# A three-stage decode kernel on one Trainium2 core: decode operations spread over three engines, a new tabulated order, and places for the attention steps of later blocks

## The chip, the cores and the metric

The kernel runs on one core of a Trainium2 chip. The engines are TensorE (PE, matmuls; PEld is its weight load), VectorE (DVE), ScalarE (ACT), GpSimd (POOL) and SyncE (SP, which issues all DMA transfers here). The metric is device time in microseconds, from runs of the whole program: a median of 605.21 us in three runs before the change (604.71 to 607.05).

## The reference

A chunked, decaying linear attention gives x of 3072 tokens by 256, and two feed-forward nets follow:

```
for c in chunks:                       # per batch (4) and head (8), 768 positions
    cum = cumsum(log(a));  M = (C @ B^T) * exp(cum_i - cum_j) * causal
    y   = M @ x + (C @ state) * exp(cum)
    state = exp(sum(log a)) * state + B^T (x * exp(cum_last - cum))
x = x.reshape(3072, 256)
x = ((x @ w1) * (x @ w2)) @ w3 @ w_out      # 256 -> 1024 -> 1024 -> 256
x = max(x @ w_in, 0)                        # 256 -> 2048
out = (x * x) @ w_out2                      # 2048 -> 256
```

The weights are float64 in memory; the rest is float32.

## The kernel before

**Tiles and stages.** The 3072 tokens are 8 blocks f of 384 positions. Attention works on 16 units u of four heads and 384 positions (four chunks of 96); block f needs units 2f (even) and 2f+1 (odd). Of a unit the kernel makes: decay (four scans on DVE, one a head, L297), lw (the last decays, L309), bd (POOL, two kinds of instruction, L315 and L322: B times decays, and the decays of the state), cb and gain (PE, L373 and L331: scores C B^T and the gain of the state), m 0 to 3 (DVE, L384: scores times decays, one a head), state (DVE, L344), carry (ACT, L355: copies the state beside x), y (PE, L391), x and xl (ACT L411, DVE L418: the result split into a high and a low part, xth and xtl). The scores of heads 0 and 1 lie in two PSUM tiles cb, those of head 2 in cbw, a buffer of the ring w that feed-forward products (pw) use too and that has three buffers, and those of head 3 in yu, of which there is one. Products of float32 are made as three matmuls (L150) from high and low parts.

**A block** has an up phase ph_a of 8 steps m and a phase ph_h of 16. In a step of ph_a stand two ab products (x w1 and x w2, 6 matmuls each), copy (ACT), mul (DVE, pr), the high part (ACT, s3h), the low part (DVE, s3l), and x2 products of three steps before. wc is the product of w3 and w_out, made once on PE (L554, 16 steps of four matmuls); x2 is pr times wc. In a step of ph_h stand the h products (x2 w_in, 6 matmuls), relu and the high part of the square (ACT), sq (the square, POOL but ACT in block 0), the low part qlo (DVE, tile s3l), and the o products of three steps before.

**Decode.** The weights come as 44 pieces of 512 KB (load, SP, L233): wo1 0 to 3 (w_out), w3 0 to 15, w1 and w2 0 to 3, wi 0 to 7 (w_in), wo 0 to 7 (w_out2). Pieces 0 and 2 of w1 and w2 are their first half of columns, 1 and 3 the second. Each piece passes high (ACT, L245), low (POOL, L249) and join (DVE, L260), which make float32 of the two words; pieces of w1, w2, wi and wo then pass hi (ACT, L267) and lo (POOL, L271), which split them. Loads wait for one of nine raw buffers, which a join frees.

**Order.** For blocks 0 and 1, units 0 to 5 and all decoding, each operation is entered in a plan with its engine and its dependencies, and the table ORDER, written out by hand in the file, sets the order in which all are issued (Plan.run). For blocks 2 to 7 the order is that of the loops: a counter of slots goes up by one in each step m of both phases (24 slots a block), and run_fill issues, in the step's middle, whatever was put at this slot. Units 6 to 15 are put there: an even unit from slot 0 of the block before the one that needs it, an odd one from slot 8, both with the same steps at 0 to 14 slots behind:

```
    for u in range(EARLY, NU):
        for i, f in unit_steps(u):
            fill.setdefault(BEGIN[u] + i, []).append(f)
```

Of the kernel before, what the change touches and what calls it, by code (L numbers as in the profile page):

```python
# [5 lines left out]
F32 = mybir.dt.float32  # L6
# [40 lines left out]
BEGIN = {u: (u // 2 - 1) * (M1 + M2) + 8 * (u % 2) for u in range(EARLY, NU)}  # L47

ORDER = [
# [30 lines left out]
class Plan:  # L80
# [9 lines left out]
    def run(self, order):  # L90
        names, done = list(self.ops), set()
        assert sorted(order) == list(range(len(names)))
        for n in order:
            _, after, fn, _, _ = self.ops[names[n]]
            assert all(d in done for d in after), (names[n], [d for d in after if d not in done])
            fn()
            done.add(names[n])
# [3 lines left out]
def mixer_kernel(ctx, tc, a, bct, xb, cst, *rest):  # L101
# [42 lines left out]
    def f32(t):  # L144
        return t.bitcast(F32)
# [678 lines left out]
```

## Time and profile before

| | |
|---|---|
| median of three runs | 605.21 us (604.71 to 607.05) |
| the profiled execution | 609.12 us |
| its span, first to last instruction | 607.0 us |
| busy PE, DVE, ACT, POOL | 566.3, 317.4, 279.5, 206.5 us |
| PE's granted clock, mean over the span | 0.974 |

Durations and waits below are of the profiled execution. A busy share is a mean over stages: the first hundred microseconds, with loads and decoding, and the blocks behind them have different limits. PE's durations overlap, since matmuls are pipelined; what one costs is the distance between two starts. An idle time is shown in brackets with what ended it. A granted clock of 1.00 is 2.4 GHz and one of 0.50 is 1.2 GHz.

### The profile page before, as it was taken

Reading aid. Unit: us, or ns where it says so; the run is one execution under the profiler, and the core shown is the slowest. Engines: PE = TensorE matmul, PEld = TensorE weight load, DVE = VectorE, ACT = ScalarE, POOL = GpSimd, SP = SyncE. Lnnn points to the kernel's source line nnn. Section 1 sums busy time; section 2 is a strip of 40 time slices with the busy share of each in tenths; the row PEclk is TensorE's granted clock in tenths of the full one; section 3 lists DMA queues with packets and bytes.
Section 4 is the critical chain, followed back from the end, with each engine's and each line's share of the span. In section 5 each row is a group of like instructions: output and inputs, shape, how many; then the busy total and the mean of one; then the engine's idle time right before and its main releaser. Section 6 shows DMA issues by size and latency. Waiting matters only on the chain. (4 is left out here: it accounts for less than half of the span.)

```text
span 607.0 us, 11321 instructions
## 1 busy us (share of the span) xinstructions
PE 566.3 (93%) x4376; PEld 536.6 (88%) x4376; DVE 317.4 (52%) x564; ACT 279.5 (46%) x586; POOL 206.5 (34%) x279
## 2 busy tenths in 40 slices
PE   3589999899999998999989998999989998999997
PEld 1477788899999998999889998999879998999997
DVE  4798898453433446635373446535383446523331
ACT  2456654794344434453255424443255424443443
POOL 3778968440034112531063113421053113420242
PEclk7589999899999999999999999999999999999999
DMA  7998865201120000220022100220021200000000
GB/s 204 326 329 283 264 198 166 85 2 44 62 66 1 26 2 4 77 80 27 1 80 64 42 1 23 58 79 26 2 79 50 57 1 2 1 1 27 0 2 26
DMA packets 21020, 43.51 MB, mean 72 GB/s; under 512 B 7608, under 2 KB 10920, under 8 KB 20968
## 3 DMA queue, kind: packets, MB, share of 16 engines
q1 hardware_dynamic: 20968, 42.81, 22.4%
q8 instruction: 34, 0.56, 0.4%
q14 instruction: 18, 0.15, 0.1%
HBM read 39.55 MB, written 3.25 MB: 71 GB/s over the span
## 5 line engine op out<-in xcount | busy, mean ns | idle before, releaser
L509 POOL TENSOR_TENSOR q<-r 128x384 f32<-128x384 f32 x112 | 100.3, 900 | 274.9 <-ACT r L501 256.6
L516 DVE TENSOR_TENSOR s3l<-q,s3h 128x384 fp32r<-128x384 f32 x128 | 80.2, 633 | 139.4 <-POOL q L509 106.2
L150 PE MATMUL acc<-s3h,wo 128*128 128x384 f32 x512 | 133.4, 342 | 0.0
L501 ACT ACTIVATE r<-pw 128x384 f32<-128x384 f32 x128 | 62.1, 487 | 113.3 <-PE pw L150 112.6
L150 PEld LDWEIGHTS acc<-s3h,wo 128*128 128x128 f32 x512 | 92.8, 189 | 1.7
L150 PE MATMUL pw<-x2h,wih 128*128 128x384 f32 x256 | 87.5, 342 | 6.9 <-DVE la L384 4.6
L150 PE MATMUL acc<-s3l,wo 128*128 128x384 f32 x256 | 86.8, 339 | 0.6 <-DVE s3l L516 0.6
L150 PE MATMUL pw<-x2h,wil 128*128 128x384 f32 x256 | 86.7, 339 | 0.0
L150 PE MATMUL pw<-x2l,wih 128*128 128x384 f32 x256 | 85.2, 340 | 0.0
L467 DVE TENSOR_TENSOR pr<-pw,asb 128x384 f32<-128x384 f32 x64 | 35.6, 556 | 75.0 <-PE pw L150 73.8
L513 ACT ACTIVATE s3h<-r 128x384 fp32r<-128x384 f32 x128 | 67.1, 525 | 9.2 <-PE acc L150 4.6
L473 ACT CAST s3h<-pr 128x384 fp32r<-128x384 f32 x64 | 32.8, 513 | 71.2 <-DVE pr L467 68.0
L150 PEld LDWEIGHTS pw<-x2h,wih 128*128 128x128 f32 x256 | 48.2, 188 | 9.1 <-DVE la L384 6.2
L463 ACT COPY asb<-pw 128x384 f32<-128x384 f32 x64 | 30.7, 479 | 49.4 <-PE pw L150 49.3
L297 DVE TENSOR_TENSOR_SCAN la<-la,cs 112x384 f32<-112x384 f32 x48 | 50.3, 1054 | 0.3 <-DMA la<-az 0.3
L150 PEld LDWEIGHTS acc<-s3l,wo 128*128 128x128 f32 x256 | 48.3, 189 | 1.3 <-DVE s3l L516 1.0
L150 PEld LDWEIGHTS pw<-x2h,wil 128*128 128x128 f32 x256 | 48.4, 189 | 0.0
L150 PEld LDWEIGHTS pw<-x2l,wih 128*128 128x128 f32 x256 | 48.2, 189 | 0.0
L476 DVE TENSOR_TENSOR s3l<-pr,s3h 128x384 fp32r<-128x384 f32 x64 | 36.7, 574 | 20.1 <-ACT s3h L473 20.0
L150 PE MATMUL acc<-s3l,wch 128*128 128x384 f32 x128 | 43.4, 339 | 1.4 <-DVE s3l L476 1.4
L150 PE MATMUL pw<-xth,w2h 128*128 128x384 f32 x128 | 44.0, 344 | 0.2
L150 PE MATMUL acc<-s3h,wch 128*128 128x384 f32 x128 | 43.9, 343 | 0.0
(85 smaller groups left out, 1031.4 us busy)
## 6 DMA issues: line engine op xcount, KB each, us to landing
la<-az SPq DMA_DIRECT2D x12, 679.0 KB, 4.7
rawl<-in_wo SPq DMA_DIRECT2D x10, 512.0 KB, 5.0
rawe<-in_w3t SPq DMA_DIRECT2D x9, 512.0 KB, 6.5
xa<-in_xb SPq DMA_DIRECT2D x16, 288.0 KB, 5.3
rawl<-in_w3t SPq DMA_DIRECT2D x7, 512.0 KB, 5.9
out_t<-o SPq DMA_DIRECT2D x16, 192.0 KB, 1.9
rawl<-in_w_in SPq DMA_DIRECT2D x5, 512.0 KB, 5.5
rawl<-in_w SPq DMA_DIRECT2D x5, 512.0 KB, 7.3
```

The source lines that it names most:

```text
L150: nc.tensor.matmul(ps, lhsT=w[i == 1], rhs=x[i == 2], start=first and i == 0, stop=last and i == 2)
L297: nc.vector.tensor_tensor_scan(la[:, 0:TB], src[:, 0:TB], cs, 0.0, ALU.mult, ALU.add)
L463: nc.scalar.copy(ab[m], ab.pop((m, 0)))
L467: nc.vector.tensor_tensor(pr, ab.pop((m, 1)), ab[m], op=ALU.mult)
L473: nc.scalar.copy(pt[f, m][0], ab[m])
L476: nc.vector.tensor_tensor(pt[f, m][1], ab.pop(m), f32(pt[f, m][0]), op=ALU.subtract)
L501: nc.scalar.activation(hr[m], hp.pop(m), AF.Relu)
L509: nc.gpsimd.tensor_tensor(q, hr[m], hr[m], op=ALU.mult)
L513: nc.scalar.activation(qt[f, m][0], hr[m], AF.Square)
L516: nc.vector.tensor_tensor(qt[f, m][1], hr.pop((m, 0)), f32(qt[f, m][0]), op=ALU.subtract)
```

## The change

Three things change together. A table MOVED names, for operations of the plan that have more than one possible engine, which it is: low may be on POOL, ACT or DVE, hi on ACT or DVE, lo on POOL or DVE, carry on ACT or POOL, sq on POOL or ACT. By it low goes to ACT 21 times and to DVE 10 times, lo 13 times and hi 4 times to DVE, carry 3 times to POOL; of block 0's squares 4 go to POOL, of block 1's 11 to ACT. ORDER is another table of the same 803 operations. And the steps of units 6 to 15 are seventeen single ones, with a table AT for even and one for odd units that gives each its slot, counted from the start of the same block.

The diff; of the tables a line stands:

```diff
@@ -44,36 +44,59 @@
 PLANNED = 2
-BEGIN = {u: (u // 2 - 1) * (M1 + M2) + 8 * (u % 2) for u in range(EARLY, NU)}
 ORDER = [
-    7, 95, 19, 258, 0, 255, 107, 287, 8, 9, 251, 260, 288, 261, 264, 253, 282, 96, 97, 265, 263, 279, 20, 21, 10, 259, 11, 98, 256, 108, 109, 292, 254,
...
+]
+
+
+MOVED = {
+    5: 1, 17: 2, 21: 2, 33: 1, 41: 1, 45: 1, 57: 1, 61: 1, 65: 1, 77: 2, 81: 1, 85: 1, 91: 1, 97: 1, 99: 1, 100:
...
+}
+
+
+AT = [
+    [0, 1, 3, 5, 5, 6, 7, 7, 7, 8, 9, 9, 11, 13, 14, 14, 14],
+    [6, 6, 13, 13, 14, 16, 18, 18, 19, 19, 19, 20, 20, 22, 22, 22, 23],
 ]
@@ -91,9 +114,12 @@
         for n in order:
-            _, after, fn, _, _ = self.ops[names[n]]
+            eng, after, fn, _, _ = self.ops[names[n]]
             assert all(d in done for d in after), (names[n], [d for d in after if d not in done])
-            fn()
+            if isinstance(eng, tuple):
+                fn(eng[MOVED.get(n, 0)])
+            else:
+                fn()
             done.add(names[n])
@@ -244,9 +272,12 @@
         nc.scalar.activation(z, z, AF.Prelu, scale=2.0 ** -112, alpha=2.0 ** 32)
-    def dec_low(key):
-        t = words[key]
-        nc.gpsimd.tensor_scalar(t[:, :, 0], t[:, :, 0], 0.876 * 2.0 ** -29, 0.49, ALU.mult, ALU.add)
+    def dec_low(key, eng):
+        t = words[key][:, :, 0]
+        if eng == "ACT":
+            nc.scalar.activation(t, t, AF.Copy, scale=0.876 * 2.0 ** -29, bias=0.49)
+        else:
+            on[eng].tensor_scalar(t, t, 0.876 * 2.0 ** -29, 0.49, ALU.mult, ALU.add)
     def dec_join(key):
@@ -261,14 +292,17 @@
         spare.append(slot.pop(key))
-    def dec_hi(key):
+    def dec_hi(key, eng):
         if key in (("wo", 0), ("wo", 4)):
             to_wo(key[1] // 4)
-        nc.scalar.copy(split_to(key)[0], stage[key].bitcast(F32))
-
-    def dec_lo(key):
+        if eng == "ACT":
+            nc.scalar.copy(split_to(key)[0], stage[key].bitcast(F32))
+        else:
+            on[eng].tensor_copy(split_to(key)[0], stage[key].bitcast(F32))
+
+    def dec_lo(key, eng):
         hi, lo = split_to(key)
-        nc.gpsimd.tensor_tensor(lo, stage.pop(key).bitcast(F32), f32(hi), op=ALU.subtract)
+        on[eng].tensor_tensor(lo, stage.pop(key).bitcast(F32), f32(hi), op=ALU.subtract)
     un = {}
@@ -426,20 +461,22 @@
     def unit_steps(u):
-
-
         return [
-            *((h, lambda h=h: u_decay(u, h)) for h in range(HG)),
-            (4, lambda: (u_lw(u), u_bd(u))),
-            (7, lambda: (u_cb(u), u_gain(u))),
-            (8, lambda: (u_m(u, 2), u_m(u, 3))),
-            (9, lambda: (u_state(u), u_m(u, 0))),
-            (10, lambda: (u_m(u, 1), u_carry(u))),
-            (12, lambda: u_y(u)),
-            (13, lambda: (u_loads(u + 2), u_x(u))),
-            (14, lambda: u_xl(u)),
+            *(lambda h=h: u_decay(u, h) for h in range(HG)),
+            lambda: u_lw(u),
+            lambda: u_bd(u),
+            lambda: (u_cb(u), u_gain(u)),
+            lambda: u_m(u, 2),
+            lambda: u_m(u, 3),
+            lambda: u_state(u),
+            lambda: u_m(u, 0),
+            lambda: u_m(u, 1),
+            lambda: u_carry(u),
+            lambda: u_y(u),
+            lambda: u_loads(u + 2),
+            lambda: u_x(u),
+            lambda: u_xl(u),
         ]
-
     pt = {}
@@ -500,10 +537,10 @@
         nc.scalar.activation(hr[m], hp.pop(m), AF.Relu)
-    def h_sq(f, m):
+    def h_sq(f, m, eng="POOL"):
         q = hr[m, 0] = sb.tile([128, FB], F32, tag="s2", name="q")[:, 0:FBS[f]]
-        if f == 0:
+        if eng == "ACT":
             nc.scalar.activation(q, hr[m], AF.Square)
@@ -603,7 +640,7 @@
         op(("high", key), "ACT", [("load", key)], lambda key=key: dec_high(key))
-        op(("low", key), "POOL", [("load", key)], lambda key=key: dec_low(key))
+        op(("low", key), ("POOL", "ACT", "DVE"), [("load", key)], lambda e, key=key: dec_low(key, e))
         ends = [("join", k) for k in pieces if k not in LAST] if key in LAST and key[0] == "wo" else []
@@ -613,8 +650,8 @@
                     after += [("hi", ("wo", key[1] // 4 * 4))]
-            op(("hi", key), "ACT", after, lambda key=key: dec_hi(key))
-            op(("lo", key), "POOL", [("hi", key)], lambda key=key: dec_lo(key), frees=[("v", ("join", key))])
+            op(("hi", key), ("ACT", "DVE"), after, lambda e, key=key: dec_hi(key, e))
+            op(("lo", key), ("POOL", "DVE"), [("hi", key)], lambda e, key=key: dec_lo(key, e), frees=[("v", ("join", key))])
     for f in range(2):
@@ -646,7 +683,7 @@
         op(("state", u), "DVE", [("cb", u)] + prev("carry") + prev("state"), lambda: u_state(u))
-        op(("carry", u), "ACT", [("state", u)], lambda: u_carry(u))
+        op(("carry", u), ("ACT", "POOL"), [("state", u)], lambda e: u_carry(u, e))
         op(("y", u), "PE", [("carry", u)] + [("m", u, h) for h in range(HG)], lambda: u_y(u),
@@ -674,7 +711,7 @@
             op(("relu", f, m), "ACT", [("h", f, m, 1)], lambda m=m: h_relu(f, m), ["s1"], [("w", ("h", f, m, 0))])
-            op(("sq", f, m), "POOL" if f else "ACT", [("relu", f, m)], lambda m=m: h_sq(f, m), ["s2"], [("s1", ("relu", f, m))])
+            op(("sq", f, m), ("POOL", "ACT")[::1 if f else -1], [("relu", f, m)], lambda e, m=m: h_sq(f, m, e), ["s2"], [("s1", ("relu", f, m))])
             op(("qhi", f, m), "ACT", [("relu", f, m)], lambda m=m: h_hi(f, m), ["s3"], [("s1", ("relu", f, m))])
@@ -705,8 +742,8 @@
     for u in range(EARLY, NU):
-        for i, f in unit_steps(u):
-            fill.setdefault(BEGIN[u] + i, []).append(f)
+        for i, f in zip(AT[u % 2], unit_steps(u)):
+            fill.setdefault((u // 2 - 1) * (M1 + M2) + i, []).append(f)
     def ph_a(f, tail):
```

**PE at the start**, from the first scan's inputs on (rows: the decays spread over the partitions; wo1v and ve: wc's inputs; bd_97 and la: of unit 0). Before:

```order
L284 MATMUL rows<-al,sel 112x388 x8
L554 MATMUL acc<-wo1v,ve 128x256 x4
L373 MATMUL cb<-ct,bt_103 112x96 x2
L373 MATMUL cbw<-ct,bt_103 112x96
L373 MATMUL yu<-ct,bt_103 112x96
...
L331 MATMUL yu<-xa,bd_97 32x32 x16
L554 MATMUL acc<-wo1v,ve 128x256 x4
L391 MATMUL yu<-la,xa 32x96 x16
L284 MATMUL rows<-al,sel 112x388 x3
```

The same place after the change:

```order
L318 MATMUL rows<-al,sel 112x388 x8
L408 MATMUL cb<-ct,bt_103 112x96 x2
L408 MATMUL cbw<-ct,bt_103 112x96
L408 MATMUL yu<-ct,bt_103 112x96
...
L365 MATMUL yu<-xa,bd_97 32x32 x16
L426 MATMUL yu<-la,xa 32x96 x16
L318 MATMUL rows<-al,sel 112x388 x3
L591 MATMUL acc<-wo1v,ve 128x256 x8
```

The whole of unit 0's cb, gain and y moved ahead of the first wc step, where one step stood before and one between.

**POOL in the first 30 us** (bd and w2s: of units 0 and 1; rawl and rawe: low; w2l: lo). Before:

```order
L271 TENSOR_TENSOR w2l<-v,w2h 128x512
L315 TENSOR_TENSOR bd_97<-xa,la 96x256
L322 COPY w2s_99<-la 16x4 x4
L249 TENSOR_SCALAR rawl<-rawl 128x512 x5
L315 TENSOR_TENSOR bd_98<-xa,la 96x256
L322 COPY w2s_100<-la 16x4 x4
L249 TENSOR_SCALAR rawe<-rawe 128x512 x3
```

After:

```order
L349 TENSOR_TENSOR bd_97<-xa,la 96x256
L356 COPY w2s_99<-la 16x4 x4
L349 TENSOR_TENSOR bd_98<-xa,la 96x256
L356 COPY w2s_100<-la 16x4 x4
L280 TENSOR_SCALAR rawe<-rawe 128x512
L280 TENSOR_SCALAR rawl<-rawl 128x512
L390 COPY xa<-st_101 16x128 x4
L280 TENSOR_SCALAR rawl<-rawl 128x512 x3
```

Both units' bd moved to the front, low words between them to other engines, and the carry of unit 0 came in.

**DVE around the end of block 2's up phase** (pr and the s3l made from it: the last steps of that phase; x2l: its result; la<-cbw, la<-yu, la<-cb: m 2, 3 and 0 or 1 of the even unit; la<-la,cs: scans of the odd one; st: state; s3l<-q: qlo). Before:

```order
L467 TENSOR_TENSOR pr<-pw,asb 128x384
L476 TENSOR_TENSOR s3l<-pr,s3h 128x384
L489 TENSOR_TENSOR x2l<-acc,x2h 128x384 x2
L384 TENSOR_TENSOR la<-cbw,la 112x384
L384 TENSOR_TENSOR la<-yu,la 112x384
L297 SCALAR_TENSOR_TENSOR la<-la,cs 112x384
L516 TENSOR_TENSOR s3l<-q,s3h 128x384
L344 SCALAR_TENSOR_TENSOR st_101<-st_101,w2s_99,yu 128x32 x4
L384 TENSOR_TENSOR la<-cb,la 112x384
L297 SCALAR_TENSOR_TENSOR la<-la,cs 112x384
L516 TENSOR_TENSOR s3l<-q,s3h 128x384
L384 TENSOR_TENSOR la<-cb,la 112x384
```

After:

```order
L331 SCALAR_TENSOR_TENSOR la<-la,cs 112x384 x2
L513 TENSOR_TENSOR s3l<-pr,s3h 128x384
L504 TENSOR_TENSOR pr<-pw,asb 128x384
L419 TENSOR_TENSOR la<-cbw,la 112x384
L419 TENSOR_TENSOR la<-yu,la 112x384
L513 TENSOR_TENSOR s3l<-pr,s3h 128x384
L526 TENSOR_TENSOR x2l<-acc,x2h 128x384 x2
L378 SCALAR_TENSOR_TENSOR st_101<-st_101,w2s_99,yu 128x32 x4
L553 TENSOR_TENSOR s3l<-q,s3h 128x384
L419 TENSOR_TENSOR la<-cb,la 112x384 x2
L553 TENSOR_TENSOR s3l<-q,s3h 128x384 x4
L331 SCALAR_TENSOR_TENSOR la<-la,cs 112x384 x2
```

The reads of cbw and yu moved ahead of x2l, and the scans moved out from between the even unit's steps, two ahead of the last steps of the up phase and two behind four qlo.

## Rows read from the trace of the kernel before

**Rows 1.** The page: the span and the number of instructions.

```profile
span 607.0 us, 11321 instructions
```

**Rows 2.** Windows: length, busy us (instructions) of each engine, granted clock, DMA.

```profile
0.00:15.00 15.00, 5.86 (x14) 2.15 (x14) 6.24 (x16) 4.12 (x6) 5.19 (x23) 0.78 0.73 203
15.00:30.00 15.00, 8.51 (x77) 6.13 (x78) 10.83 (x21) 6.68 (x11) 11.11 (x20) 0.50 0.95 326
30.00:60.00 30.00, 27.76 (x233) 22.62 (x232) 26.28 (x50) 18.35 (x36) 23.53 (x28) 0.90 0.91 305
60.00:90.00 30.00, 27.26 (x298) 23.32 (x297) 27.77 (x43) 17.91 (x36) 23.98 (x21) 1.00 0.72 231
90.00:104.42 14.42, 12.99 (x128) 11.97 (x126) 12.28 (x18) 7.11 (x14) 12.05 (x15) 1.00 0.52 161
104.42:603.60 499.18, 483.88 (x3642) 470.38 (x3632) 233.99 (x420) 224.86 (x484) 130.62 (x175) 1.00 0.11 34
```

The order of its columns is length; PE, PEld, DVE, ACT, POOL; PE's clock, the DMA engines' share, GB/s.

**Rows 3.** Waits of PE from 120 to 600 us: total, times, longest.

```profile
PE yu L391 <- DVE la L384: 5.2, 5, 1.0
PE pw L150 <- DVE la L384: 4.6, 5, 0.9
PE yu L373 <- issue: 2.5, 5, 0.5
```

**Rows 4.** Timeline of PE in block 2: start, length, instruction, [idle before it].

```profile
233.54 0.44 PE L150 MATMUL pw<-x2h,wih 128*128 128x384 f32 x1 [0.92 <-DVE la L384]
...
240.75 0.86 PE L391 MATMUL yu<-la,xa 112*32 112x96 f32 x30 [1.04 <-DVE la L384]
```

**Rows 5.** Timeline of DVE in block 2.

```profile
232.94 0.55 DVE L384 TENSOR_TENSOR la<-cbw,la 112x384 f32<-112x384 f32 x1
...
240.06 0.55 DVE L384 TENSOR_TENSOR la<-cb,la 112x384 f32<-112x384 f32 x1
...
248.40 0.54 DVE L418 TENSOR_TENSOR xtl<-yu,xth 128x384 fp32r<-128x384 f32 x1
```

**Rows 6.** Timeline of PE at the first h products of block 0.

```profile
103.06 0.34 PE L373 MATMUL cb<-ct,bt 16*112 16x96 f32 x2
...
104.42 0.45 PE L150 MATMUL pw<-x2h,wih 128*128 128x384 f32 x1
...
109.64 0.45 PE L150 MATMUL pw<-x2h,wih 128*128 128x384 f32 x1 [2.30 <-ACT r L501]
109.92 0.34 PE L150 MATMUL pw<-x2h,wil 128*128 128x384 f32 x1
110.10 0.34 PE L150 MATMUL pw<-x2l,wih 128*128 128x384 f32 x1
```

**Rows 7.** Groups by line and form: busy us, mean ns; idle time before, releasers.

```profile
L297 DVE TENSOR_TENSOR_SCAN la<-la,cs 112x384 f32<-112x384 f32 x48 | 50.3, 1054 | 0.3 <-DMA la<-az 0.3
L249 POOL TENSOR_SCALAR rawl<-rawl 128x512 uint32<-128x512 uint32 x27 | 25.6, 949 | 9.5 <-DMA rawl<-in_w3t 3.3 <-DMA rawl<-in_wo 2.0 <-DMA rawl<-in_w 1.4
L245 ACT ACTIVATE rawl<-rawl 128x512 f32<-128x512 f32 x27 | 18.2, 679 | 21.9 <-DMA rawl<-in_wo 8.1 <-DMA rawl<-in_w 5.5 <-DMA rawl<-in_w3t 4.8
L260 DVE SCALAR_TENSOR_TENSOR v<-rawl 128x512 uint32<-128x512 uint32 x17 | 15.7, 921 | 5.7 <-POOL rawl L249 2.9 <-POOL wo L271 2.5 <-POOL w1l L271 0.3
L271 POOL TENSOR_TENSOR wo<-v,wo 128x512 fp32r<-128x512 f32 x8 | 11.3, 1418 | 13.5 <-ACT wo L267 7.2 <-DVE s3l L516 6.3
L572 DVE TENSOR_TENSOR wcl<-acc,wch 128x512 fp32r<-128x512 f32 x4 | 2.6, 677 | 0.0
```

**Rows 8.** Timelines of DVE and POOL at 87 us.

```profile
87.95 1.46 DVE L260 SCALAR_TENSOR_TENSOR v<-rawl 128x512 uint32<-128x512 uint32 x1
...
87.56 1.30 POOL L271 TENSOR_TENSOR wil<-v,wih 128x512 fp32r<-128x512 f32 x1 [1.57 <-ACT wih L267]
```

**Rows 9.** DMA issues on the page: count, KB of one, us to landing.

```profile
rawl<-in_w SPq DMA_DIRECT2D x5, 512.0 KB, 7.3
```

More of the change, by code (lines that the diff above doesn't have):

```diff
@@ L142, in mixer_kernel @@
     bt = [const.tile([128, NCH, TA], F32, name=f"bt{i}") for i in range(2)]
+    on = {"POOL": nc.gpsimd, "DVE": nc.vector}
     def f32(t):
@@ L347, in u_state, with u_carry @@
             )
-    def u_carry(u):
+    def u_carry(u, eng="ACT"):
         d = un[u]
@@ L353, in u_carry @@
         c0 = NCH * ((u // 2) % 2)
+        copy = nc.scalar.copy if eng == "ACT" else on[eng].tensor_copy
         for h in range(HG):
-            nc.scalar.copy(
+            copy(
                 d["xa"][T:TA, h * NCH * D:(h + 1) * NCH * D].rearrange("p (c d) -> p c d", d=D),
```

66 rows, old and new, of tables (MOVED, ORDER) are left out of this document.

## The prediction

> **What bounds the kernel now.** Read first the windows by stage [rows 2]. From 104.42 us, where TensorE (PE) starts the first product of block 0's second feed-forward (the h products), to its last matmul it is busy 483.9 of 499.2 us at full clock: in that stretch only PE's own work and its 15.3 us of idle time count, and VectorE (DVE), ScalarE (ACT) and GpSimd (POOL) are at 47, 45 and 26%. Before 104.42 it is another kernel: PE idles 15.6 of the first 30 us, runs at a granted clock of 0.50 from 15 to 30 us, and later has short holes, while DVE is busy 26.3, 27.8 and 12.3 of 30, 30 and 14.4 us and POOL 23.5, 24.0 and 12.1; DMA brings 326 GB/s, then 305, then 231. So the start is bound by the decoding of weights on DVE and POOL, and by the loads ahead of them. A busy PE overstates work there, because ends of matmuls are modelled.
>
> Then PE's waits after 120 us [rows 3]: three kinds, five times each, 12.3 us in all. One set is seen in the timeline [rows 4]: at 233.54 a product waits 0.92 us, at 240.75 the attention's y waits 1.04 us. The DVE rows of the same time [rows 5] say why. The product waits for a PSUM buffer of the ring w that cbw holds until DVE has read it at 232.94, behind the two x2l. y waits for the last masked score, which DVE reaches at 240.06, because a scan of the next unit stands between every two steps of this unit. The third kind, 0.5 us, is cb of the odd unit, which needs the tile yu; DVE releases it with xtl at 248.40.
>
> **The change after the planned part.** The table AT gives seventeen steps of units 6 to 15 places of their own. Of an even unit, the two score products that free cbw and yu's half come right behind cb, ahead of the two x2l; its odd partner's four scans go from among its steps to slots 6 and 13; the odd cb goes from slot 15 to 18, four slots behind the even xl. All three causes are gone. What is new is two scans at slot 6 ahead of that slot's low part s3l. Their price is 2 x 1.05 us by the mean scan [rows 7]; a slot there has 18 matmuls at a spacing of 0.18 us [rows 6], 3.2 us, against DVE's 2.1 and two products of 0.55 (the rows of that size in [rows 5]). The s3l that waits is used only after the next slot's 12 products, cb and 12 more matmuls, over 5 us later. Cover: PE's work; without it 2.1 us a block, 10.5 in five. I take the removal of all 12.3 us, end to end from 0 to 13.
>
> **The change at the start.** Four things change.
>
> Work by engine up to the first x2l of block 0, counted in the two orders. POOL had 40 low, 16 lo and 6 bd; it keeps 13, 9 and 3. At 0.95 and 1.42 us [rows 7] that takes off 27 x 0.95 + 7 x 1.42 = 35.6 us. ACT gets 21 low, and three more high words, but three hi, two x and three carries fewer; low on ACT isn't in the trace, the nearest row is its own high word, 0.68 us [rows 7], and 21 x 0.68 = 14.3 us go into an engine that was busy 54 of 104 us [rows 2]. DVE gets 9 low, 8 lo, 3 hi and one join. Its lo is nearest to wcl, 0.68 us alone; a low or hi isn't in the trace at this size and lies between 0.34 (half of that row) and 0.92 (the join's mean); I take 0.6, near wcl: 9 x 0.6 + 8 x 0.68 + 3 x 0.6 + 0.9 = 13.5 us. It loses, to a later time, the scans of units 4 and 5 (8 x 1.05), two lw, the four masked scores (0.55 each) and the state of unit 3, and two xl: 14 us. So DVE's queue is not shorter by count.
>
> It is shorter by contention. A join took 1.46 us at 87.95, while POOL's subtraction of 1.30 us from 87.56 ran [rows 8]; the join's mean is 0.92 against about 0.69 for one alone (wcl's row, of the same size, is 0.68) [rows 7]. Thirty-eight joins at up to 0.24 us are 9 us; with POOL's work halved I take 5, from 0 to 9. The Trainium skill ("SBUF — State Buffer", Who interferes with whom) states that DVE and GpSimd share a port pair which is an exclusive lock, taken by a DVE instruction with two SBUF inputs against a GpSimd one that reads, and that the loser waits for the whole instruction. By that rule the 1.46 is 0.9 of waiting and the join after it, as the row has it; it also speaks against the change, since the lo moved to DVE has two SBUF inputs too and is locked by what POOL keeps. That is the third rival.
>
> Loads and order. Attention's inputs now come first: unit 0's cb needs them, and it no longer stands behind four wc matmuls. wc (the product of w3 and w_out) follows as its pieces land; the second half of w1 and w2 comes later, the last piece of w2 as load 36 of 44 instead of 24. Loads are 512 KB [rows 9]: 36 are 18.9 MB, and with 29 transfers of 24 KB, four of 288 KB, and the small ones 21 MB are ahead. By 30 us the old order had moved 15 us x 203 GB/s + 15 us x 326 GB/s = 7.9 MB [rows 2]; the other 13.1 MB at 326 to 305 GB/s take 40 to 43 us, so that piece lands at 70 to 73 us. Its decode is two words on ACT, a join, hi, and lo on POOL: 0.68 + 0.68 + 0.69 + 0.6 + 1.42 = 4.1 us, with queueing 5 to 8. So the first product that needs it starts at 75 to 81 us. Behind it stand, up to the first h product, 7 x 6 matmuls of ab and 12 x 3 of x2, 78 x 0.18 = 14 us, and one y of 0.86: 90 to 96 us. Check by DVE: 83.4 us busy before 104.42 now, less 5 for contention, is 78; idle time of 13 us in the first 30 should fall to about 8, since the eight scans of units 0 and 1, which stood among joins, now come nearly in a row and need no weights; 8 us of later idle time are filled or kept: 86 to 94 us. I take **93 us for the first h product**, instead of 104.42, with bounds of 86 and 104.
>
> What this pays back. Unit 3's cb and y and unit 4's cb go behind the first h product: two times 1.36 us (103.06 to 104.42) and 0.86 [rows 4, 6] = 3.6 us of PE work. DVE, ACT and POOL had 53, 55 and 74% idle after 104.42, so the moved scans and scores are hidden there; in block 0's h products ACT carries most squares; four go to POOL, and eleven of block 1 come from POOL to ACT, at no price, since PE had no wait there [rows 3, 4]. Three carries go from ACT to POOL, where the trace has none: between no change and 1.42 us more each (POOL's longest row here), inside the 2 us below. Loads behind unit 4's ct and bt wait for cb of unit 2, about 75 us; they are the last three pieces and are wanted only by late h and o products. The 2.30 us wait at 109.64 [rows 6] can stay or go; I leave 2 us of idle time for it and for others of the planned part, between 0 and 6.
>
> **Sum.** 93 + 483.9 of PE work + 3.6 + 2 + a tail of 3.4 (607.0 - 603.6) [rows 1, 2, 6] = 585.9 us of span. The profiled execution was 609.12 us with a span of 607.0, so 2.1 lie around it; it was 3.9 above the median of 605.21. 585.9 + 2.1 - 3.9 = **584 us**, 3.5% faster. A measurement of this kernel tells about 0.5% from no change, 3 us.
>
> **Rivals.** First, only the attention steps pay: the first h product stays at 104.42, as DVE's queue is as long as before by count; the 3.6 us moved behind it were saved ahead of it only if PE was the bound there, which it wasn't. Then 605.2 - 12.3 + 3.6 = 596.5. For it speaks DVE's 93% busy share from 60 to 90 us; against it that POOL's 35.6 us are taken off a chain in which joins wait for POOL.
>
> Second, only the start pays: slot 6's two scans, slowed by bd on POOL as the join of [rows 8] was by a subtraction (each by 0.8 us), push the s3l and the next mul behind them past their cover, and each block waits about 2.5 us again, at another place: 584 + 12 = 596.
>
> Third, slower. PE's new order puts the last four wc steps behind the fifth ab product, which needs a PSUM buffer that the first mul frees, and in DVE's order seven low, two lo and four more joins than before stand ahead of that mul. If those of DVE's 20 new instructions that meet POOL take the 1.46 us of the locked join [rows 8] instead of 0.6, and the 38 joins keep their contention, DVE gains 20 x 0.86 = 17 us and loses none of the 5: 93 + 17 + 5 = 115, with the qlo of block 0 late by 6 us as well: 584 + 22 + 6 = 612. It decides against the change once the first h product comes later than 104.42 + 12.3 - 3.6 = 113 us. POOL keeps 13 x 0.95 + 9 x 1.42 = 25 us of decoding in some 90, so by its share one instruction in four meets one, and I take the case as unlikely. The Trainium skill ("SBUF — State Buffer", Who interferes with whom) would have each that meets wait to the end of the other.
>
> Fourth, the steps do nothing measurable: gains of one part eaten by the other, 602 to 608. The orders as built show that both parts do move, so it is no more than a sum that happens to cancel.
>
> **Chances.** Both parts 0.64 (574 to 596), attention alone 0.13, start alone 0.09, cancelling 0.06, slower 0.08. Faster by over 0.5%: 0.86; within: 0.06; slower: 0.08. The range runs from 86 us for the first h product with no idle time left (93 - 86 + 2 = 9 less: 575) to beyond the two single cases: 573 to 600.
>
> **What would show it.** Right: PE's first h product near 93; DVE's joins near 0.7 us; POOL under 40 us busy before it; no wait of PE for la after 230 us, and windows of 10 us full at 230 to 250. Wrong: DVE casts and subtractions of 1.2 us and more; PE waiting for s3l or pr at a block's end; a second stretch of clock 0.50; a load of w2 that lands after 80 us.

## The result and the profile after

The changed kernel takes **579.66 us** (median of four runs, 578.59 to 580.40), against 605.07 us of the kernel before on the same chip (604.71 to 607.05): a ratio of 0.957, with a 95% interval of 0.9545 to 0.9599. The prediction was 584 us, 573 to 600. The profiled execution took 580.4 us.

The page of after, span and busy shares (its rows answer to [rows 1]):

```profile
span 578.5 us, 11305 instructions
PE 558.3 (97%) x4376; PEld 534.1 (92%) x4376; DVE 319.9 (55%) x591; ACT 288.7 (50%) x598; POOL 152.8 (26%) x240
```

Windows of after, with the columns of [rows 2] (length; PE, PEld, DVE, ACT, POOL; PE's clock, DMA share, GB/s). The cut at 94.59 us is block 0's first h product, as 104.42 was before:

```profile
0.00:15.00 15.00, 7.90 (x16) 3.10 (x16) 10.13 (x24) 4.83 (x7) 4.43 (x24) 1.00 0.75 225
15.00:30.00 15.00, 10.06 (x108) 7.91 (x109) 10.17 (x22) 6.29 (x12) 8.28 (x15) 1.00 0.95 355
30.00:60.00 30.00, 25.26 (x200) 20.55 (x199) 25.84 (x49) 20.00 (x38) 8.91 (x11) 1.00 0.90 297
60.00:90.00 30.00, 30.00 (x211) 28.79 (x210) 26.63 (x47) 25.10 (x46) 11.31 (x14) 0.94 0.76 250
90.00:94.59 4.59, 4.59 (x54) 4.19 (x54) 3.80 (x8) 4.38 (x9) 2.56 (x2) 1.00 0.03 12
94.59:574.90 480.31, 480.31 (x3796) 469.55 (x3792) 243.34 (x446) 227.61 (x489) 117.29 (x177) 1.00 0.13 37
```

PE is full from 60 us on; before, it had holes up to 104 us and behind. POOL's work ahead of the first h product fell from 75.9 us (the first five rows of [rows 2]) to 35.5. DVE and ACT are nearly full from 60 to 90 us, at 26.6 and 25.1 of 30.

All waits of PE in after from 0 to 120 us over 1.5 us in all (total, times, longest). From 120 us on the same view is empty, where [rows 3] had 12.3 us:

```profile
PE cb L408 <- DMA ct<-in_bct: 3.8, 1, 3.8
PE yu L426 <- POOL xa L390: 3.6, 3, 2.3
PE rows L318 <- DVE la L333: 3.3, 6, 1.0
PE pw L178 <- DVE w1l L305: 1.8, 1, 1.8
```

**Where the time went.** The start of each phase is its first product in the timeline of PE. Cut there, the two profiles (spans 607.0 and 578.5) compare so; the last column is what the prediction's terms make of each stretch:

| stretch | before | after | difference | predicted |
|---|---|---|---|---|
| up to the first h product | 104.42 | 94.59 | -9.8 | -11.4 |
| blocks 0 and 1 from there, to block 2's first ab product | 100.44 | 100.33 | -0.1 | +2.6 (3.6 + 2 - 3.0 of idle there) |
| the five h phases of blocks 2 to 6 | 189.05 | 170.59 | -18.5 | -12.3 |
| all else | 213.09 | 212.99 | -0.1 | 0 |
| sum | 607.0 | 578.5 | -28.5 | -21.1 |

The h phase of blocks 2 to 6 took 37.62 to 37.64 us before (once 38.53) and takes 34.10 to 34.13 us now. The up phases between them stay as they were, at 30.08 and 30.09 us.

**What of the table is one execution's.** The profiled execution of before was 3.9 us above its median, so the 28.5 us here are 25.4 by the medians. Its blocks 0 and 1 hold the wait of 2.30 us of [rows 6]. The experiments below have four more profiles with the order and engines of before (at_only, at_a, at_b, at_c): that wait is 0.5 to 1.9 us there, blocks 0 and 1 take 97.8 to 98.7 us, and the first h product comes at 101.57 to 104.54. Of the kernels with after's order and engines up to the first h product, after, no_at, no_sq and bt_late (with one load moved) have it at 92.80 to 94.59 and take 100.3 to 100.4 us for blocks 0 and 1. So the change costs these blocks 1.6 to 2.6 us, near the 2.6 predicted; the -0.1 of the table hides it.

### The profile page after: what moved, and what is told of

It is laid out like the page before. It is cut to its first block, busy times and chain, and to the rows that moved or that the text cites. A ratio compares the mean times of both kernels' runs of the same rounds, so it can differ in the third digit from the quotient of the medians.

```text
span 578.5 us, 11305 instructions
## 1 busy us (share of the span) xinstructions
PE 558.3 (97%) x4376; PEld 534.1 (92%) x4376; DVE 319.9 (55%) x591; ACT 288.7 (50%) x598; POOL 152.8 (26%) x240
## 4 chain that ended last, share of the span: by engine, by line
PE 92%; DMA 5%; DVE 1%; SPq 1%; POOL 0%; ACT 0%; issue 0%; DVEq 0%; ACTq 0%; POOLq 0%
PE pw L178 47%; PE acc L178 36%; DMA rawe<-in_w3t 4%; PE acc L591 3%; PE cb L408 2%; PE yu L426 2%; PE yu L365 1%; DMA ct<-in_bct 1%; POOL xa L390 0%; PE yu L408 0%; DVE ve L291 0%; DVE w1l L305 0%; SPq L228 0%; PE rows L318 0%; DVE la L419 0%
## 5 line engine op out<-in xcount | busy, mean ns | idle before, releaser
L546 POOL TENSOR_TENSOR q<-r 128x384 f32<-128x384 f32 x105 | 90.8, 868 | 228.2 <-ACT r L538 203.4
L553 DVE TENSOR_TENSOR s3l<-q,s3h 128x384 fp32r<-128x384 f32 x128 | 77.8, 616 | 115.0 <-POOL q L546 91.4
L331 DVE TENSOR_TENSOR_SCAN la<-la,cs 112x384 f32<-112x384 f32 x48 | 48.0, 1022 | 0.4 <-DMA la<-az 0.4
L349 POOL TENSOR_TENSOR bd<-xa,la 96x256 f32<-96x256 f32 x16 | 12.9, 809 | 127.9 <-DVE la L343 117.4
L178 PE MATMUL pw<-xth,w1l 128*128 128x384 f32 x128 | 43.7, 342 | 1.8 <-DVE w1l L305 1.8
```

The costliest lines, as they stand in the source:

```text
L178: nc.tensor.matmul(ps, lhsT=w[i == 1], rhs=x[i == 2], start=first and i == 0, stop=last and i == 2)
L331: nc.vector.tensor_tensor_scan(la[:, 0:TB], src[:, 0:TB], cs, 0.0, ALU.mult, ALU.add)
L349: nc.gpsimd.tensor_tensor(bd[u % 2][:, 0:HC * N].rearrange("p (h c n) -> p h c n", h=HG, n=N), d["xa"][0:T, HC * D:].rearrange("p (h c n) ...
L546: nc.gpsimd.tensor_tensor(q, hr[m], hr[m], op=ALU.mult)
L553: nc.vector.tensor_tensor(qt[f, m][1], hr.pop((m, 0)), f32(qt[f, m][0]), op=ALU.subtract)
```

## Experiments

Each kernel differs from the changed one in its tables alone; most have one or two of them as in before. With all three put back (ORDER of before, MOVED empty, BASE for AT) the instructions stand as before. BASE is the old slots written as a table:

```
BASE = [[0, 1, 2, 3, 4, 4, 7, 8, 8, 9, 9, 10, 10, 12, 13, 13, 14],
        [8, 9, 10, 11, 12, 12, 15, 16, 16, 17, 17, 18, 18, 20, 21, 21, 22]]
```

Its places are, in order: four scans, lw, bd, cb with gain, m 2, m 3, state, m 0, m 1, carry, y, loads, x, xl. Line numbers differ a little from kernel to kernel; the names don't.

### One table at a time

**at_only**: the old order and engines, with the new AT.

```diff
-AT = BASE
+AT = [[0, 1, 3, 5, 5, 6, 7, 7, 7, 8, 9, 9, 11, 13, 14, 14, 14],
+      [6, 6, 13, 13, 14, 16, 18, 18, 19, 19, 19, 20, 20, 22, 22, 22, 23]]
```

> The kernel before with the new places of the attention steps of units 6 to 15 alone; order and engines of the planned part as before. Theory A: what a wait costs is the distance between two starts of PE, not the idle time shown, so the five h phases of blocks 2 to 6 fall from 37.6 us (38.5 in one) to about 34.1, and the gain is 17 to 18.5 us: 587 to 588 us. Theory B (the prediction's count): the idle time shown, 12.3 us, is the gain: 593 us, with h phases of about 35.2 us. The first h product of block 0 stays at 104.4 us.

587.42 us, ratio 0.9695 (0.9676 to 0.9713): 18.5 us less than the 605.93 of before beside it. As theory A said, all h phases of blocks 2 to 6 are at 34.10 to 34.14 us, PE's view of waits after 120 us is empty, and the first h product stays at 104.54. So the table alone gives 18.5 us, not 12.3.

**no_at**: the changed kernel with BASE.

```diff
-AT = [[0, 1, 3, 5, 5, 6, 7, 7, 7, ...
+AT = BASE
```

> The changed kernel with the old places of the attention steps of units 6 to 15; new order and new engines stay. Theory A: the start and blocks 0 and 1 give some 10 us, so 595 us; h phases of blocks 2 to 6 at 37.6 us again. Theory B: the planned part gives 13 us: 592 us. A third possibility, that the two parts depend on one another, would show as gains of this run and the run with the places alone that do not add up to 25.4 us.

597.88 us, ratio 0.9861 (0.9843 to 0.9880): 8.1 us less than before, where 10 or 13 was expected. The first h product is at 92.80, the h phases at 37.6 to 37.7 us again. The parts add up: 18.5 + 8.1 = 26.6, against 25.9 for both (4.28% of 605.93).

**no_moved**: the new order and AT, all operations on their old engines.

```diff
-MOVED = {5: 1, 17: 2, 21: 2, 33: 1, ...}
+MOVED = {}
```

> The changed kernel, new order and new places, with every decode operation, carry and square on its old engine (low and lo on GpSimd, hi and carry on ScalarE). Theory A (the engines matter): 64 operations that the order expects on other engines come back to GpSimd, 31 low of 0.95 us and 13 lo of 1.42 us are 48 us more on it in the first 95 us, so GpSimd is the bound; the first h product comes at 105 to 115 us instead of 94.6 and the time is 590 to 600 us. Theory B (the order matters, the engines hardly): under 2 us from the changed kernel, 580 to 582 us.

585.75 us, ratio 0.9665 (0.9649 to 0.9681), between the two theories and 1.7 us better than at_only (585.02 to 586.13 against 586.52 to 588.78). Of the 66 entries that leave MOVED, the 31 low, the 13 lo and 11 squares come back to POOL, which is busy 72.2 us in the first 105. The first h product comes at 96.93, 7.6 us ahead of at_only's, but blocks 0 and 1 take 102.97 us from there, against 98.70 in at_only and 100.33 in after.

**moved_only**: the old order and BASE, with the new engines.

```diff
-MOVED = {}
+MOVED = {5: 1, 17: 2, 21: 2, 33: 1, ...}
```

> The kernel before with the new engines alone; its old order and old places stay. Theory A (engines and order belong together): the old order lets attention of units 3 to 5 and late loads stand where they were, GpSimd's relief shortens joins, but the first h product moves by under 4 us: 600 to 606 us. Theory B (contention and GpSimd are the bound at the start): the first h product moves by 6 to 10 us: 595 to 599 us. It is slower than before if operations that come to VectorE and ScalarE in the old order delay what stands behind them there.

609.01 us, ratio 1.0055 (1.0033 to 1.0077): 3 us slower than before, and worse than either theory. The first 105 us in windows, of before and of moved_only:

```profile
0.00:105.00 105.00, 82.96 (x747) 66.78 (x748) 83.99 (x146) 54.25 (x102) 76.06 (x106) 0.87 0.78 252
```

```profile
0.00:105.00 105.00, 82.53 (x753) 67.04 (x753) 87.58 (x166) 60.69 (x110) 42.12 (x78) 0.89 0.79 255
```

POOL was relieved by 34 us, as planned, and nothing came of it; in an order made for the old engines DVE got 3.6 us more work and ACT 6.4. That this is what costs the 3 us is not shown: the profiled execution was the shortest of ten (606.10 us), and its first h product comes at 103.44.

**The start's gain belongs to the pair.** The engines alone cost 3 us, the order alone gives 1.7 (no_moved against at_only), both together 8.1 (no_at).

**Faster joins or another order?** The prediction made DVE's queue shorter by contention: joins that no longer wait for POOL. The windows of the joins' line alone, up to the first h product (length; DVE's busy us and number of joins; clock, DMA share, GB/s), are of before, at_only, no_moved, moved_only and after:

```profile
0.00:104.42 104.42, 30.86 (x37) 0.87 0.78 252
0.00:104.54 104.54, 34.13 (x37) 0.98 0.79 252
0.00:96.93 96.93, 33.24 (x38) 0.88 0.79 260
0.00:103.44 103.44, 28.26 (x37) 0.88 0.79 255
0.00:94.59 94.59, 25.40 (x38) 0.98 0.80 266
```

In this stretch at_only is the kernel before, so the first two rows differ by execution alone. With the new order and the old engines (third row) the joins are as slow as ever, and the first h product, at 96.93, still comes 4.6 us or more ahead of all five profiles of the old one. With the new engines in the old order (fourth) the joins are faster by 3 to 6 us, and it comes at the usual time, 103.44. With both it comes another 2 to 4 us earlier. So the relief of the joins, which the prediction sized well at 5 us, buys nothing by itself, and the larger part of the gain up to there is the order's. Whether the other 2 to 4 us come of the joins or of the rest of the work taken off POOL isn't shown: in low_only below the joins take 29.01 us, and the product comes at 93.72.

### Which slots of AT pay

**at_a** puts only m 2 and m 3 of the even unit behind its cb, **at_b** moves only the odd unit's four scans, **at_c** only shifts the odd unit by one slot from cb on. Each is before with one kind of place changed. The places of at_b and at_c are not those of the new table, which has the odd scans at 6 and 13 and the odd cb at 18. The edits, in this order:

```diff
-        [0, 1, 2, 3, 4, 4, 7, 8, 8, 9, 9, 10, 10, 12, 13, 13, 14],
+        [0, 1, 2, 3, 4, 4, 7, 7, 7, 9, 9, 10, 10, 12, 13, 13, 14],
```

```diff
-        [8, 9, 10, 11, 12, 12, 15, 16, 16, 17, 17, 18, 18, 20, 21, 21, 22]
+        [4, 5, 6, 7, 12, 12, 15, 16, 16, 17, 17, 18, 18, 20, 21, 21, 22]
```

```diff
-        [8, 9, 10, 11, 12, 12, 15, 16, 16, 17, 17, 18, 18, 20, 21, 21, 22]
+        [8, 9, 10, 11, 12, 12, 16, 17, 17, 18, 18, 19, 19, 21, 22, 22, 23]
```

> The kernel before with one of the new places alone: the even unit's score products of heads 2 and 3 (which free cbw and half of yu) right behind its cb, slot 7 instead of 8. Theory A (distance between starts): the wait of 1.07 us a block at the third h product goes, 5.4 us in five: 600 to 601 us, h phases of blocks 2 to 6 at 36.5 us. Rival: the two products of 0.55 us come out of the queue behind x2l only, and y's wait grows or stays, since VectorE's queue up to y holds the same work: the h phase gains less than 0.5 us a block: 604 us.

> The kernel before with the four scans of the odd unit alone moved, from slots 8 to 11 to slots 4 to 7, so that none stands between the even unit's steps. Theory A: y's wait of 1.34 us a block goes, and the odd cb's wait of 0.7 us with it if VectorE reaches xtl earlier: 6.7 to 10 us in five: 596 to 599 us. Rival: a scan in each of slots 4 to 7 delays the low part and the mul there, PE waits in the up phase (30.1 us a block now) by as much as it gains: 605 us.

> The kernel before with the steps of the odd unit from cb on one slot later (16 to 23 instead of 15 to 22). Theory A: cb then finds yu free, and 0.7 us a block go, 3.5 us in five: 602 us. Rival: xtl of the odd unit, one slot later, comes too late for the first ab product of the next block, and the up phase gains what the h phase loses: 605 us.

| kernel | us (before beside it 604.62) | ratio (95%) | an h phase of blocks 2 to 6, against 37.63 |
|---|---|---|---|
| at_a | 598.55 | 0.9901 (0.9883 to 0.9919) | 36.44, 1.19 less |
| at_b | 596.93 | 0.9870 (0.9850 to 0.9889) | 35.87 to 35.91, 1.76 less |
| at_c | 600.22 | 0.9927 (0.9903 to 0.9951) | 36.72, 0.92 less |

One of the five h phases is 0.9 us longer in each of the three, as in before. What is left of the three kinds of [rows 3], from 120 to 575 us: at_a, then at_b, then at_c. PE pw is the h product that waits for cbw; yu <- DVE la is y; yu <- issue is the odd cb.

```profile
PE yu L408 <- DVE la L401: 5.2, 5, 1.0
PE yu L390 <- issue: 2.6, 5, 0.5
```

```profile
PE pw L160 <- DVE la L401: 4.6, 5, 0.9
PE yu L408 <- DVE la L401: 0.8, 4, 0.2
```

```profile
PE yu L408 <- DVE la L401: 5.2, 5, 1.0
PE pw L160 <- DVE la L401: 4.6, 5, 0.9
```

Each edit takes away the wait whose cause it removes and leaves the others; of y's, at_b leaves 0.8 of 5.2 us. at_b removes the odd cb's too: without the scans in between, xl comes early enough for it. By the medians the three give 6.1, 7.7 and 4.4 us, at_a and at_c some 2 us more than expected. So the causes are those that the prediction named, and their prices are larger than the waits show. at_a's kind showed 0.92 us a block and paid 1.19, at_c's showed 0.5 and paid 0.92. The three gains sum to 3.87 a block against 3.5 together, since at_b and at_c both remove the third kind.

Why they are larger stands in the timeline of before, in the rows just ahead of the waiting ones, which are in [rows 4] for the first two kinds:

```profile
232.29 0.34 PE L150 MATMUL pw<-x2h,wil 128*128 128x384 f32 x1
...
239.36 0.35 PE L391 MATMUL yu<-la,xa 112*32 112x96 f32 x2
...
248.27 0.26 PE L373 MATMUL cbw<-ct,bt 16*112 16x96 f32 x1
249.04 0.30 PE L373 MATMUL yu<-ct,bt 16*112 16x96 f32 x1 [0.51 <-issue]
```

The row just behind the first waiting one:

```profile
233.82 0.34 PE L150 MATMUL pw<-x2h,wil 128*128 128x384 f32 x1
```

From 232.29 to the start at 233.54 are 1.25 us, where PE's usual spacing is 0.18: 1.07 lost, 0.92 shown. From 239.36 to 240.75 it is 1.39, with some 0.05 for the small matmuls between: 1.34 lost, 1.04 shown. From 248.27 to 249.04 it is 0.77, some 0.7 lost, 0.51 shown. The sum is 3.1 us a block, of the 3.5 measured. The idle time begins at the modelled end of the last matmul, and that end lies behind the point at which the next could have started. The other 0.4 us lies in the distances just behind the waits, which are wider than usual too: from 233.54 to 233.82 are 0.28. Summed over all starts of one h phase (block 3), the distances between products, within y and around cb are 1.20, 1.48 and 0.81 us longer in before than in at_only, 3.5 in all.

### Which of the moved operations pay

**low_only**: only the 31 low moved; hi, lo, carries and squares on their old engines. **carry_act**: only the three carries back on ACT. **no_sq**: only the 15 squares back. All with the new order and AT. What leaves MOVED in each, in this order:

```diff
-99: 1, 100: 1, 106: 1, 118: 1, 136: 1, 141: 1, ... 788: 1, 795: 1,
```

```diff
-275: 1, 331: 1, 385: 1,
```

```diff
-513: 1, 541: 1, 597: 1, 611: 1, 697: 1, 711: 1, 732: 1, ... 795: 1,
```

> The changed kernel with the low words alone on their new engines (21 on ScalarE, 10 on VectorE); lo, hi, carries and squares on the old ones. Theory A (low is the larger part of GpSimd's relief, 29 of 48 us): the first h product within 1 us of the changed kernel's, and most of the 6 us that all engines together give: 580 to 582 us. Theory B (each lo on GpSimd, 1.42 us and last before a product, is what PE waits for): 584 to 586 us.

581.50 us beside 606.27 of before, ratio 0.9606 (0.9573 to 0.9640); first h product at 93.72. Against no_moved (0.9665) and the whole change (0.9572), moving low is about two thirds of what MOVED brings; the intervals are too wide for a closer figure. Up to the first h product low gives all of it; blocks 0 and 1 take 102.30 us from there against 100.33.

> The changed kernel with the three carries (units 0, 2 and 4) back on ScalarE. On GpSimd the first took 3.12 us, on ScalarE one takes 1.25, and y of unit 0 waited 3.6 us for it. Theory A (the start is bound by loads and the decode behind them): y of unit 0 comes 2 us earlier and nothing else does, under 1 us of difference: 579 to 580.5 us. Theory B (attention's first chain is on the path): 2 us less, 577.5 us. Slower only if ScalarE's 1.25 us delays squares of blocks 0 and 1: 581 us.

580.75 us beside 604.62, ratio 0.9603 (0.9585 to 0.9622), no gain, and near the 581 expected if ACT is delayed; first h product at 93.68, and blocks 0 and 1 take 102.03 us from there instead of 100.33. The timelines tell why: PE of carry_act in block 1's h phase, ACT of carry_act there, and ACT of after at the same place.

```profile
161.78 0.34 PE L172 MATMUL pw<-x2l,wih 128*128 128x384 f32 x1
163.24 0.44 PE L172 MATMUL pw<-x2h,wih 128*128 128x384 f32 x1 [1.13 <-ACT r L532]
```

```profile
161.04 1.22 ACT L384 COPY xa<-st 16x128 f32<-16x128 f32 x4
162.29 0.52 ACT L538 ACTIVATE q<-r 128x384 f32<-128x384 f32 x1
162.72 0.47 ACT L532 ACTIVATE r<-pw 128x384 f32<-128x384 f32 x1
```

```profile
161.53 0.51 ACT L544 ACTIVATE q<-r 128x384 f32<-128x384 f32 x1
161.94 0.47 ACT L538 ACTIVATE r<-pw 128x384 f32<-128x384 f32 x1
```

The copy of 1.22 us stands between two relus, the relu comes late, and the h product that needs its PSUM buffer waits 1.13 us (1.28 by the starts: 163.24 less 161.78 less 0.18). low_only and no_moved, which also have the carries on ACT, show the same wait, at 0.7 us. In after the last one is on POOL and PE doesn't wait. The early carry pays nothing that shows. On POOL it is long, and unit 0's y waits 2.3 us for it (the wait for xa in the list of after above), but in carry_act y waits 2.2 us for the copy on ACT; the first h product there is at 93.68, within what two profiles of one order differ by (92.8 to 94.6).

> The changed kernel with the squares of blocks 0 and 1 on their old engines (ScalarE all 16 of block 0, GpSimd all 16 of block 1), the rest as in the changed kernel. The prediction's count: no price, as PE has no wait there: 579 to 580.5 us. Rival: without any new engine the h phases of blocks 0 and 1 took 2.6 us more, and if that came from the squares this run is at 582 us.

579.85 us beside 606.27, ratio 0.9573 (0.9549 to 0.9596): the same as the change. The squares are free.

### A hole in the loads

**bt_late**: after has 2 us with hardly a load, from 32 to 34 us, in which SP waits before a small load (bt of unit 3, whose buffer is not free). That load is moved behind the next six weight loads (the expectation counts five).

```diff
-... 229, 301, 343, 61, 116, 60, ... 300, 108, 340, 42, 2,
+... 229, 301, 61, 116, 60, ... 300, 108, 340, 343, 42, 2,
```

> The changed kernel with one DMA in another place of the order: the load of head 3's B of unit 3 (it waits for cb of unit 1) stands behind the load of the second half of w2's first columns instead of ahead of a w3 piece, five weight loads later. In the changed kernel SyncE stood before it from 29.5 to 32.9 us and DMA moved 25 GB/s from 32 to 34 us. Theory A (loads bound the start): about 2.5 us of idle DMA go, the weights behind it land earlier, the first h product comes at 92 us instead of 94.6, and the time is 577 to 578 us. Theory B (the decode queues bound it): VectorE reaches nothing earlier, under 0.5 us: 579.2 to 580.2 us.

579.51 us beside 606.27, ratio 0.9566 (0.9543 to 0.9590): no gain. Two windows of after, then two of bt_late:

```profile
32.00:34.00 2.00, 2.00 (x68) 1.79 (x63) 1.20 (x3) 0.01 (x1) 0.00 (x0) 1.00 0.09 25
34.00:36.00 2.00, 2.00 (x11) 1.74 (x11) 1.89 (x7) 1.35 (x3) 0.00 (x0) 1.00 0.74 226
```

```profile
32.00:34.00 2.00, 2.00 (x68) 1.79 (x69) 1.04 (x2) 0.00 (x0) 0.08 (x1) 1.00 0.67 249
34.00:36.00 2.00, 2.00 (x11) 1.77 (x10) 1.89 (x7) 1.20 (x2) 0.00 (x0) 1.00 0.43 127
```

The hole is filled (25 to 249 GB/s), and another opens right behind it (226 to 127): the loads sent early use up the nine raw buffers, and SP waits for the next join instead.

## Why the prediction held, and where it was off

**The causes were right for the waits and, in part, for the start.** Both parts pay, and the parts add up (at_only, no_at). "Attention alone", "start alone", "cancelling" and "slower" each have a run against them: no_at, at_only, and the change itself; slot 6's two scans, which "start alone" rests on, cost nothing, since PE has no wait after 120 us and the up phases stay at 30.08. Each of the three waits goes with its named cause (at_a, at_b, at_c). At the start the prediction named the order and the relief of the joins side by side; the runs show that the order gives more and that the relief alone gives nothing (the windows of the joins above).

**The start, by its own steps.** The chain of the last piece of w2 came out nearly as reckoned. Its load was issued at 66.14 us and landed 6.7 later, at 73 (70 to 73 predicted). SP's timeline in after, then the list of DMA issues from 50 to 95 us, where it is the only one of its tile (count, KB, us to landing), then the timelines of POOL and PE with its lo and the first product that needs it:

```profile
66.14 0.42 SPq L261 DMA_DIRECT2D rawe<-in_w  x1
```

```profile
rawe<-in_w SPq DMA_DIRECT2D x1, 512.0 KB, 6.7
```

```profile
78.27 1.47 POOL L305 TENSOR_TENSOR w2l<-v,w2h 128x512 fp32r<-128x512 f32 x1 [3.19 <-ACT w2h L299]
```

```profile
79.86 0.45 PE L178 MATMUL pw<-xth,w2h 128*128 128x384 f32 x1
...
94.59 0.44 PE L178 MATMUL pw<-x2h,wih 128*128 128x384 f32 x1
```

79.86 lies in the predicted 75 to 81, and 14.7 us of products follow, where 14 + 0.86 was the estimate: 94.59 against 93. In the first 30 us DVE idles 9.7 (8 predicted, 13 before), and it is busy 76.6 us up to the first h product (78 predicted). POOL's 35.5 us are under the 40 named as a sign, no load of w2 lands after 80 us, and no window of after shows the clock of 0.50 again.

**The prices on other engines.** Groups of after up to 120 us, line and engine, form, count | busy us, mean ns | idle before:

```profile
L278 ACT ACTIVATE rawe<-rawe 128x512 uint32<-128x512 uint32 x13 | 8.8, 676 | 2.1 <-DMA rawe<-in_wo 2.0
L280 DVE TENSOR_SCALAR rawl<-rawl 128x512 uint32<-128x512 uint32 x7 | 4.5, 646 | 0.6 <-DMA rawl<-in_w 0.5
L301 DVE CAST wih<-v 128x512 fp32r<-128x512 f32 x2 | 0.8, 423 | 0.0
L305 DVE TENSOR_TENSOR wil<-v,wih 128x512 fp32r<-128x512 f32 x6 | 4.2, 699 | 0.1
L305 DVE TENSOR_TENSOR w1l<-v,w1h 128x512 fp32r<-128x512 f32 x2 | 2.4, 1195 | 0.0
L390 POOL COPY xa<-st 16x128 f32<-16x128 f32 x8 | 5.0, 630 | 2.5 <-DVE st L378 2.1
```

low on ACT is 0.68 us, as taken from its high word. low on DVE is 0.65 in this row and hi 0.42, where 0.6 was taken for both; lo is 0.70 against 0.68. The joins up to the first h product came down from 0.83 and 0.92 us each (30.86 and 34.13 for 37) to 0.67 (25.40 for 38), near the 0.7 named as a sign. The four copies of a carry took 3.12, 2.27 and 1.99 us on POOL in the three units, and take 1.25 on ACT: 0.7 to 1.9 us more, where 0 to 1.42 was allowed, so only the first lay outside.

**The lock exists and decides little.** Of the 20 operations that are new on DVE up to the first h product, four took over 0.1 us longer than alone while POOL worked: one subtraction of 1.70 us, and three low of 0.85, 0.88 and 1.50, against 0.69 and 0.43 alone; 3 us in all. The two long ones, in the timelines of DVE and POOL, and PE behind the subtraction:

```profile
57.20 1.70 DVE L305 TENSOR_TENSOR w1l<-v,w1h 128x512 fp32r<-128x512 f32 x1
...
70.91 1.50 DVE L280 TENSOR_SCALAR rawl<-rawl 128x512 uint32<-128x512 uint32 x1
```

```profile
57.08 1.27 POOL L305 TENSOR_TENSOR w2l<-v,w2h 128x512 fp32r<-128x512 f32 x1 [3.22 <-DVE la L331]
...
70.66 1.47 POOL L305 TENSOR_TENSOR wil<-v,wih 128x512 fp32r<-128x512 f32 x1 [1.75 <-ACT wih L299]
```

```profile
58.95 0.44 PE L178 MATMUL pw<-xth,w1l 128*128 128x384 f32 x1 [1.81 <-DVE w1l L305]
```

DVE's subtraction took 1.70 us instead of 0.69, and PE waited 1.81 us for it. That is the slower rival's mechanism: its 0.86 us more is near the 1.0 of these two, but it needed all 20, and four of 20 is near the one in four that the prediction gave as POOL's share. The Trainium skill ("SBUF — State Buffer", Who interferes with whom) has the engine that issues second wait for the whole instruction of the other; by that rule DVE's would be 1.15 us of waiting (58.35 less 57.20) and 0.69 of work, 1.84, and the row has 1.70, so it agrees within 0.15. The same sum for the join of [rows 8] is 0.91 and 0.69, 1.60 against the row's 1.46.

Before had such a meeting in a late block: the one h phase of 38.53 us. A low part there took 1.17 us, where 0.56 is usual, beside a square on POOL, and PE waited 0.63 us for it. at_a, at_b and at_c have it too; at_only, no_at, moved_only and after have not.

```profile
440.22 1.17 DVE L516 TENSOR_TENSOR s3l<-q,s3h 128x384 fp32r<-128x384 f32 x1 [2.27 <-POOL q L509]
```

**The mis-sized term.** The sum was 7.4 us of span too long (585.9 against 578.5). The removal of the three waits was put at the idle time shown, 12.3 us, and gave 18.5 (at_only; by the profiles five times 3.5, and 0.9 for the block just told): this is the step that failed, and 0 to 13 was no bound. The other two terms of the table hold better than it says. The first h product, 93, came at 94.59 in this execution and at 92.80 to 94.59 in four kernels with the same start. Blocks 0 and 1, 2.6 us more, took 1.6 to 2.6 more than in the four other profiles with the order of before; the -0.1 came of the long wait in the one that was profiled. So start and deferred work were to give 8.8 us together, and no_at gives 8.1. With the carries on ACT blocks 0 and 1 take 102 to 103 us from the first h product (carry_act, low_only, no_moved). The late carry on POOL gives 1.7 back in that stretch; the medians have 1.1, within their intervals.

**Still open.** What binds the start between 30 and 65 us in the changed kernel. In after's chain of work that ended last two loads of w3 stand there (6.83 us from 37.90 and 8.90 us from 44.79), and behind them the subtraction of 57.20. bt_late shows that one hole in the loads is not it. More raw buffers weren't tried.

## What to carry to other kernels

Price a wait of PE by the distance between the starts around it, less the usual spacing, and not by the idle time shown: here the distances gave 3.1 us a block, and 3.5 with the wider ones behind each wait, which is what the change saved; the idle time showed 2.5. An assignment to engines and an issue order are one decision: engines without the order cost 3 us, the order without the engines gave 1.7, both gave 8. On an engine that feeds TensorE's PSUM buffers, look for the one long small operation between two short ones; a copy of 1.2 us between two relus made TensorE wait 1.1 us (1.3 by the starts) while ACT was half idle.

## What the runs showed of the hardware

**A cast on DVE is quick.** One of 128x512 from float32 took 0.42 us in the mean, and a low of every second word at its fastest 0.43, while a join of the same size with two inputs takes 0.68. The three low that met POOL took 0.85 to 1.50. From the timeline of DVE:

```profile
39.88 0.43 DVE L280 TENSOR_SCALAR rawl<-rawl 128x512 uint32<-128x512 uint32 x1
```

**A small copy on POOL is dear, and uneven.** Four copies of 16x128 took 3.12 us at 21.11 in after, 2.27 at 85.79 and 1.99 at 161.15; ACT's four took 1.2.

**A half clock at the start of the new order cost nothing.** From 15 to 30 us PE's granted clock was 0.50 before [rows 2], which is the lower of the two levels, 1.2 GHz; it was 1.00 in after. The change could owe its start to that; these runs speak against it. In no_at and no_sq, with the start of after, it was 0.56 and 0.55, and the first h product came at 92.80 and 93.50; in after and bt_late it was 1.00, and the product came at 94.59 and 93.14. The window of no_at:

```profile
15.00:30.00 15.00, 10.11 (x111) 8.08 (x112) 9.96 (x22) 6.23 (x11) 8.35 (x15) 0.56 0.97 357
```

PE was 10.1 us busy there in both, waiting for inputs the rest of the time; its speed wasn't what the start waited for. For the order of before, where the first h product comes at 101.57 to 104.54, no pair of runs settles this.
